# Rows of scores loaded in two parts, eight heads a round ahead, in a one-core talking-heads attention with a gated feed-forward behind it

## The chip, the core and the metric

The kernel runs on one core of a Trainium2 chip. The metric is the time of one execution on the device, in microseconds. TensorE does the matmuls and transposes, VectorE (DVE) and ScalarE (ACT) evict PSUM and do the element-wise work, GpSimd (POOL) helps, and SyncE (SP) issues nearly all DMA transfers, one after the other in the order of the program.

## The reference

Four batches, 12 heads, 448 rows, head size 64; then 1792 tokens through a feed-forward of 768 to 2048 to 768.

```python
scores = scale * np.matmul(q, k.transpose(0, 1, 3, 2))
scores = np.einsum('bhij,hg->bgij', scores, w_pre)
scores = scores - np.max(scores, axis=-1, keepdims=True)
attn = np.exp(scores)
attn = attn / (np.sum(attn, axis=-1, keepdims=True) + 1e-09)
attn = np.einsum('bhij,hg->bgij', attn, w_post)
attn_out = np.matmul(attn, v)
x = attn_out.transpose(0, 2, 1, 3).reshape(B * S, H * D)
h = x @ w_in
g = np.where(h >= 1, h, np.where(h <= -1, 0.0, (h + 1) ** 2 / 4))
out = g @ w_out
```

The two small matrices w_pre and w_post mix heads, so that the heads of one row of q must come together.

## The kernel before

**Attention, the first 440 us.** The rows of q are cut into 16 tiles: four a batch, of 120, 120, 120 and 88 rows. `scores` (L169) multiplies q and k for four heads of a tile at a time and evicts them to `ssb[t]`, which holds [row, head, column] for the whole tile; VectorE evicts two of the four heads (L187), ScalarE the other two (L189). A tile so takes three calls: heads 0 to 3, 4 to 7, 8 to 11.

To mix heads by a matmul, heads must lie on partitions. A *block* is 10 rows of a tile (a few have 9), taken with a stride. `load_s` (L198) moves one block by a DMA from SBUF to SBUF, from 10 partitions that hold 12 heads each to 120 partitions (row, head) of 448 columns:

```python
x = ap_.tile([KM, S], F32, tag="s10", name="s10", bufs=8)
nc.sync.dma_start(out=x[:ni * H], in_=ssb[t][o:n:nb])
```

`pre` (L214) multiplies the block by `wpre`, a 120x120 matrix with w_pre on ten diagonal places, either as one fp32 matmul (L223) or, for blocks that VectorE has split into a high and a low half (`split`, L205), as three faster ones (L221). A tile has 12 blocks, or 9 for the tile of 88 rows, in three *groups* of 4 (or 3): 48 groups. `row_max` (VectorE, L226), `exps` (ScalarE, L232), `norm` (GpSimd, L238 and L243, with a reciprocal on VectorE, L239) and `post` (TensorE, L260, evicted at L262) follow for each block, and `pv` (L296) multiplies by v.

**The loop (L893)** goes through the groups. Its round n, in program order, which is also the order of each engine's queue: load the rows of group n+1 (odd blocks first); "pre" of group n; the transposes planned in `at` (q and, at a batch's turn, k); the loads planned in `mid` (q, k) and the load of raw feed-forward weights (`conv_load`); the row maxima; the split of the first odd block of group n+1; `visit` (pv of an older tile); the exponentials; norm; copies of transposed q and k (`ql`, L166, reads the transposes' PSUM bank); the second split; "post" of group n-1; the conversion of weights (L373 to L377); the store of the weights converted a round ago (`conv_store`, L381); the score matmuls planned in `vis`; and what is planned in `late` (loads of q, load of the next batch's v, L130 and L133; the store of x, L340).

The score matmuls of tile t stand at the ends of rounds 3t-4, 3t-3 and 3t-2. The first group of tile t, group 3t, is loaded in round 3t-1 and is needed there by the first split: its rows can be moved only when the last four heads are evicted. k of the next batch is loaded in rounds 6 to 8 of each twelve and transposed a round later (L141, L149); v of the next batch is loaded in rounds 13 to 15 and the like. The PSUM pool `ps_l` has six banks in rotation, and s10 has eight buffers.

**The start (L758)** loads q, k, the head matrices and all three parts of v of batch 0, computes the scores of tile 0 and part of tile 1, makes `wpre`, `wpost` and the high and low halves of wpre on VectorE (L813 to L821), from a mask that GpSimd makes (L777 to L782), and enters the loop. Buffers of v's parts hold k's raw rows of batch 0 before.

**The feed-forward, from about 440 us to the end,** is not touched.

Of the kernel before, what the change touches and what calls it, by code (L numbers as in the profile page):

```python
# [9 lines left out]
F32 = mybir.dt.float32  # L10
# [12 lines left out]
def tile_talking_heads_moe(  # L23
# [11 lines left out]
    nc = tc.nc  # L35
# [159 lines left out]
    wr = {}  # L195
    aT = {}

    def load_s(m):  # L198
        t, o, ni, c = blocks[m]
        n, nb = tiles[t][2:]  # L200
        x = ap_.tile([KM, S], F32, tag="s10", name="s10", bufs=8)
        nc.sync.dma_start(out=x[:ni * H], in_=ssb[t][o:n:nb])
        s10[m] = x

    def split(m):  # L205
        k = blocks[m][2] * H
# [7 lines left out]
    def pre(m):  # L214

        k = blocks[m][2] * H
        lps[m] = ps_l.tile([KM, S], F32, tag="l", name="ps_l")
        x = s10.pop(m)
        if isinstance(x, tuple):
            for j, (w, y) in enumerate(((wpre_h, x[0]), (wpre_l, x[0]), (wpre_h, x[1]))):  # L220
                nc.tensor.matmul(out=lps[m], lhsT=w[:k], rhs=y[:k], start=(j == 0), stop=(j == 2))  # L221
        else:
            nc.tensor.matmul(out=lps[m], lhsT=wpre[:k], rhs=x[:k], start=True, stop=True)  # L223

    def row_max(m, nm):
        nc.vector.tensor_reduce(out=nm, in_=lps[m], axis=AX.X, op=ALU.max, negate=True)  # L226
# [156 lines left out]
    def conv(n, f):  # L383
        if n in CS and CS.index(n) < 2 * NF:
            f(CS.index(n))
# [372 lines left out]
    with tc.manual_schedule():  # L758
# [10 lines left out]
            load_k(0, hp, k0[hp // 2])  # L769
        load_q(1)  # L770
        wrep = ap_.tile([KM, H, IB], F32, tag="wr", name="wrep", bufs=8)
        wrep = wrep.rearrange("p h i -> p (h i)")[:, :2 * H].rearrange("p (n h) -> p n h", n=2)
        for n, w in enumerate((w_pre, w_post)):
            nc.sync.dma_start(out=wrep[:, n, :], in_=w.unsqueeze(0).to_broadcast([IB, H, H]))
        make_identity(nc, ident)

        mask = ap_.tile([KM, H, IB], F32, tag="wr", name="mask", bufs=8)[:, 0, :]  # L777
        nc.gpsimd.memset(mask, 1.0)
        nc.gpsimd.affine_select(out=mask, in_=mask, compare_op=ALU.is_ge, fill=0.0,
                                base=0, pattern=[[-H, IB]], channel_multiplier=1)  # L780
        nc.gpsimd.affine_select(out=mask, in_=mask, compare_op=ALU.is_ge, fill=0.0,
                                base=H - 1, pattern=[[H, IB]], channel_multiplier=-1)  # L782

        ps_w = pair()

# [8 lines left out]
        trans_q(0, 1)()()  # L794
        warm(4)
        trans_k(0, 1)()()
        for g in range(3):
            scores(0, [2 * g, 2 * g + 1], g == 1)
            if g < 2:
                for hp in range(2 * g + 2, 2 * g + 4):  # L800
                    trans_k(0, hp)()()
        for g in range(3):
            load_v(0, g)
        for g in range(2):
            trans_q(1, g)()()
        for m in groups[0]:
            load_s(m)
        wpre = ap_.tile([KM, KM], F32, name="wpre", bufs=1)
        wpost = ap_.tile([KM, H, IB], F32, name="wpost", bufs=1)
        wpre_h = ap_.tile([KM, KM], F32R, name="wpre_h", bufs=1)  # L810
        wpre_l = ap_.tile([KM, KM], F32R, name="wpre_l", bufs=1)

        nc.vector.scalar_tensor_tensor(  # L813
            out=wpre.rearrange("p (i g) -> p i g", g=H),
            in0=mask.unsqueeze(2).to_broadcast([KM, IB, H]), scalar=float(D) ** -0.5,
            in1=wrep[:, 0, :].unsqueeze(1).to_broadcast([KM, IB, H]), op0=ALU.mult, op1=ALU.mult)
        nc.vector.tensor_tensor(
            out=wpost, in0=wrep[:, 1, :].unsqueeze(2).to_broadcast([KM, H, IB]),
            in1=mask.unsqueeze(1).to_broadcast([KM, H, IB]), op=ALU.mult)
        nc.vector.tensor_copy(out=wpre_h, in_=wpre)  # L820
        nc.vector.tensor_tensor(out=wpre_l, in0=wpre, in1=wpre_h.bitcast(F32), op=ALU.subtract)  # L821
        scores(1, [0, 1], True)
        scores(1, [2, 3])
        at = {}
        mid = {}
        late = {}
# [3 lines left out]

        vis = {}
        vis2 = {}
        for g in range(2):
            put(0, lambda g=g: load_q(2, (g,)))
        for t in range(1, len(tiles)):
# [57 lines left out]
        for n in range(NG + 2):  # L893
            if n == NE:
                s_qk.close()
                s_se.close()
                pool['w'] = ctx.enter_context(tc.tile_pool(name="ffw", bufs=2, side="right",
                                                           reuse_waits="tile"))
                pool['ps_h'] = ctx.enter_context(tc.tile_pool(
                    name="ps_h", bufs=1, space=PSUM, side="right", reuse_waits="tile"))  # L900
            if n == NG - 1:
                s_ss.close()
            ms = groups[n] if n < NG else ()
            old = list(groups[n - 1]) if 0 < n <= NG else []
# [12 lines left out]
            for f in mid.pop(n, ()):  # L917
                f()
            conv(n + 1, conv_load)
            for m in ms:  # L920
                row_max(m, nm[:, m - ms[0]:m - ms[0] + 1])
            if n == NG - 1:
                w0_lo()
            if nxt:
                split(nxt.pop(0))
            rests = list(old)
            early = n < NE
            copies = visit(n, rests) if early else ()
            for j, m in enumerate(ms):
                if j == 3 and old and not early:  # L930
                    post(old.pop(0))
                exps(m, j, sm)
            conv(n, conv_scaled)
            if ms:
                norm(ms, sm)
            for f in (*turned, *copies):
                f()
            for m in nxt:
                split(m)
            if n == NG:  # L940
                step(0)
            for m in old:
                post(m)
            conv(n, conv_rest)
            conv(n - 1, conv_store)
            if not early:
                for f in visit(n, rests):
                    f()
            for t, hps in vis.pop(n, ()):
                scores(t, hps)  # L950
            for f in late.pop(n, ()):
                f()
# [155 lines left out]
```

## Time and profile before

| | |
|---|---|
| Timed executions | 870.63, 877.53 and 877.32 us; median 877.32 |
| The profiled execution | 873.21 us, of which the span (first to last instruction) is 871.5 |
| Mean granted TensorE clock | 0.998 |
| Busy share of the span | TensorE 98%, VectorE 74%, ScalarE 65%, GpSimd 24% |
| DMA | 162.47 MB, mean 186 GB/s |

A row of a timeline or wait view names the engine, the line of the kernel, the operation and the tiles (out<-in); a time in brackets is how long the engine sat idle just before, and what it was released by. SPq is SyncE's queue: its rows give the time in which transfers were issued, not in which they ran. PEld is the weight load of TensorE. In a table by windows, an engine's column is its busy time, and the PEclk column is the granted clock, where 1.00 is 2.4 GHz and 0.50 is 1.2 GHz.

### The profile page before, as it was taken

The page shows a single profiled execution, that of the slowest core. Times are in us where ns is not written, and L with a number is a line of the kernel's source. Part 1 is how long each engine was busy: PE and PEld are TensorE (multiplying, and loading weights), DVE is VectorE, ACT ScalarE, POOL GpSimd, SP SyncE. Part 2 cuts the span into 40 slices and gives each one's busy share as a digit, 9 for nine tenths or more (in the row PEclk, how much of TensorE's full clock was granted, in tenths as well). Part 3 has the DMA queues.
Part 4 walks back from the last instruction along what each step waited for, and adds up shares of the span by engine and source line. Part 5 has one row for each costly group of instructions (what it writes and reads, how often), then busy time and mean ns, then how long its engine had stood idle before and what let it go on. Part 6 is the DMA issues. An engine that isn't in the chain of part 4 may idle for free.

```text
span 871.5 us, 19952 instructions
## 1 busy us (share of the span) xinstructions
PE 854.1 (98%) x7848; PEld 734.2 (84%) x7848; DVE 645.1 (74%) x938; ACT 565.2 (65%) x1171; POOL 212.4 (24%) x269
## 2 busy tenths in 40 slices
PE   8999999999999999899999999999999999999998
PEld 6678777778787787687778788899999999999998
DVE  4887577775777767768578977997668978777853
ACT  3778788787887778778666466676667434433431
POOL 0366245653356533457320000000000000000000
PEclk9999999999999999999999999999999999999999
DMA  7888679986699876897556655654435544123331
GB/s 162 235 233 231 200 202 259 280 242 197 194 264 274 252 214 162 258 272 252 192 168 177 241 181 179 212 181 127 127 109 163 170 157 137 55 90 111 109 128 63
DMA packets 155329, 162.47 MB, mean 186 GB/s; under 512 B 66916, under 2 KB 148964, under 8 KB 155236
## 3 DMA queue, kind: packets, MB, share of 16 engines
q1 hardware_dynamic: 152404, 160.51, 61.1%
q8 instruction: 62, 1.02, 0.5%
q10 hardware_dynamic: 2832, 0.69, 0.4%
q14 instruction: 31, 0.25, 0.1%
HBM read 88.81 MB, written 33.82 MB: 141 GB/s over the span
## 4 chain that ended last, share of the span: by engine, by line
PE 86%; DMA 6%; DVE 3%; ACT 2%; SPq 2%; issue 1%; ACTq 0%; POOL 0%; DVEq 0%
PE ps_f L712 23%; PE ps_f L547 21%; PE ps_a L260 10%; PE ps_l L223 8%; PE ps_q L311 5%; DMA s<-ssb 5%; PE ps_l L221 5%; PE ps_q L180 3%; PE ps_s L180 3%; PE ps_r L276 2%; PE ps_q L306 1%; DMA k<-in_k_dram 1%; PE ps_t L161 1%; PE ps_k L141 1%; SPq L133 1%
## 5 line engine op out<-in xcount | busy, mean ns | idle before, releaser
L243 POOL TENSOR_SCALAR wr<-wpost,rs 120x120 f32<-120x120 f32 x180 | 141.4, 801 | 63.5 <-DVE rs L239 47.5
L232 ACT ACTIVATE e<-ps_l,nm 120x448 f32<-120x448 f32 x180 | 112.4, 632 | 60.9 <-DVE nm L226 59.6
L260 PE MATMUL ps_a<-wr,e 120*64 120x120 f32 (+1 forms) x2160 | 118.9, 266 | 0.0
L226 DVE TENSOR_REDUCE nm<-ps_l 120x1 f32<-120x448 f32 x180 | 105.7, 619 | 15.6 <-PE ps_l L223 11.4
L260 PEld LDWEIGHTS ps_a<-wr,e 120*64 120x64 f32 x2160 | 110.2, 137 | 2.6 <-issue 2.6
L695 ACT ACTIVATE sgh_p<-gq_p 128x1024 fp32r<-128x1024 f32 (+1 forms) x56 | 53.3, 953 | 89.7 <-PE ps_f L712 89.5
L223 PE MATMUL ps_l<-s,wpre 120*120 120x448 f32 x196 | 94.9, 569 | 5.8 <-DMA s<-ssb 3.8
L439 DVE SCALAR_TENSOR_TENSOR wl<-wi,wh 128x768 fp32r<-128x768 f32 x71 | 67.8, 954 | 41.9 <-ACT wh L436 41.9
L712 PE MATMUL ps_f<-wh,sgh_p 128*128 128x384 f32 x294 | 98.2, 334 | 0.0
L712 PE MATMUL ps_f<-wh,sgl_p 128*128 128x384 f32 x294 | 98.2, 334 | 0.0
L712 PE MATMUL ps_f<-wl,sgh_p 128*128 128x384 f32 x294 | 98.2, 334 | 0.0
L436 ACT ACTIVATE wh<-wi 128x768 fp32r<-128x768 f32 x71 | 59.7, 842 | 57.9 <-DVE wi L659 18.0
L262 ACT ACTIVATE aT<-ps_a 128x360 f32<-128x360 f32 x180 | 80.7, 494 | 13.7 <-PE ps_a L260 4.7
L696 DVE TENSOR_TENSOR sgl_p<-gq_p,sgh_p 128x1024 fp32r<-128x1024 f32 (+1 forms) x56 | 60.9, 1089 | 35.7 <-ACT sgh_p L695 35.7
L210 DVE CAST sh<-s 120x448 fp32r<-120x448 f32 (+1 forms) x82 | 33.2, 405 | 56.5 <-DMA s<-ssb 56.3
L187 DVE COPY ssb<-ps_q 120x896 f32<-120x896 f32 (+1 forms) x46 | 49.9, 1085 | 26.7 <-PE ps_q L180 26.7
L189 ACT ACTIVATE ssb<-ps_s 120x448 f32<-120x448 f32 (+1 forms) x96 | 47.2, 547 | 20.2 <-PE ps_s L180 17.8
L377 POOL TENSOR_TENSOR wt<-wt,wk 128x768 int32<-128x768 int32 x32 | 58.3, 1821 | 7.7 <-ACT wk L373 7.7
L221 PE MATMUL ps_l<-sh,wpre_h 120*120 120x448 f32 (+1 forms) x82 | 59.1, 721 | 0.0
L712 PEld LDWEIGHTS ps_f<-wh,sgl_p 128*128 128x128 f32 x294 | 55.2, 188 | 0.0
L712 PEld LDWEIGHTS ps_f<-wh,sgh_p 128*128 128x128 f32 x294 | 55.2, 188 | 0.0
L712 PEld LDWEIGHTS ps_f<-wl,sgh_p 128*128 128x128 f32 x294 | 55.2, 188 | 0.0
(235 smaller groups left out, 1943.3 us busy)
## 6 DMA issues: line engine op xcount, KB each, us to landing
s<-ssb SPq DMA_DIRECT2D x172, 210.0 KB
wraw<-in_moe_w_in_dram SPq DMA_DIRECT2D x16, 768.0 KB
wraw<-in_moe_w_out_dram SPq DMA_DIRECT2D x16, 768.0 KB
wi<-wod SPq DMA_DIRECT2D x29, 384.0 KB
wi<-wsd SPq DMA_DIRECT2D x28, 384.0 KB
wsd<-wt SPq DMA_DIRECT2D x16, 384.0 KB
wod<-wt SPq DMA_DIRECT2D x16, 384.0 KB
wi<-wss SPq DMA_DIRECT2D x16, 384.0 KB
```

The costliest lines, as they stand in the source:

```text
L221: nc.tensor.matmul(out=lps[m], lhsT=w[:k], rhs=y[:k], start=(j == 0), stop=(j == 2))
L223: nc.tensor.matmul(out=lps[m], lhsT=wpre[:k], rhs=x[:k], start=True, stop=True)
L226: nc.vector.tensor_reduce(out=nm, in_=lps[m], axis=AX.X, op=ALU.max, negate=True)
L232: nc.scalar.activation(out=e, in_=ps, func=AF.Exp, bias=nm, accum_out=sm[:, j:j + 1])
L243: nc.gpsimd.tensor_scalar_mul(out=w[:, :, :ni], in0=wpost[:, :, :ni], scalar1=rs[:, j:j + 1])
L260: nc.tensor.matmul(out=ps[half[s], r, :ni * H], lhsT=e[:, c0:c0 + 64], rhs=w[:, :, :ni], start=True, stop=True)
L262: nc.scalar.activation(out=a[:, :, :, c:c + ni], in_=ps[:, :, :ni * H].rearrange("q r (h i) -> q r h i", h=H), func=AF.Copy)
L436: nc.scalar.activation(out=hi, in_=t, func=AF.Copy, scale=2.0 ** -8)
L439: nc.vector.scalar_tensor_tensor(out=lo, in0=t, scalar=2.0 ** -8, in1=hi.bitcast(F32), op0=ALU.mult, op1=ALU.subtract)
L547: nc.tensor.matmul(out=o, lhsT=u[:, c, k], rhs=x, start=first and r == 0 and m == 0, stop=r == 2 and m == 2, skip_group_check=True)
L696: nc.vector.tensor_tensor(out=lo, in0=src, in1=hi.bitcast(F32), op=ALU.subtract)
L712: nc.tensor.matmul(out=o, lhsT=x[:, f, c], rhs=y[:, f % 2, :], start=first and f == 0 and m == 0, stop=hf == 1 and f == 3 and m == 2, skip ...
```

## The change

The *lead* groups are the first of each tile (0, 3, 6 and so on).

- A block of a lead group is loaded by two transfers: heads 0 to 7 (80 partitions) at the end of round 3t-2, behind that round's stores and loads, and heads 8 to 11 (40 partitions) at the place of the old load, in round 3t-1. All other groups are loaded as before.
- As the order of rows on the partitions is another one there, lead groups have a `wpre` of their own, made from two more loads of parts of w_pre (each some KB) and a mask of two more patterns, with halves of its own. The splits of both are made after the first scores of tile 1 and no longer before them.
- `conv_store` is written ahead of the row maxima, and what is in `late` ahead of the exponentials (up to round 43).
- At the start, only the first part of v is loaded before the loop; the other two are loaded in rounds 3 and 4, ahead of q's load.

```diff
-    def load_s(m):
+    lead = set(m for g in range(0, NG, 3) for m in groups[g])
+    EH = 8
+    EP = EH * IB
+
+    def load_s(m, early=False):
         t, o, ni, c = blocks[m]
         n, nb = tiles[t][2:]
-        x = ap_.tile([KM, S], F32, tag="s10", name="s10", bufs=8)
-        nc.sync.dma_start(out=x[:ni * H], in_=ssb[t][o:n:nb])
-        s10[m] = x
+        if m not in s10:
+            s10[m] = ap_.tile([KM, S], F32, tag="s10", name="s10", bufs=8)
+        x = s10[m]
+        if m not in lead:
+            nc.sync.dma_start(out=x[:ni * H], in_=ssb[t][o:n:nb])
+        elif early:
+            nc.sync.dma_start(out=x[:EP], in_=ssb[t][o:n:nb, :EH])
+        else:
+            nc.sync.dma_start(out=x[EP:], in_=ssb[t][o:n:nb, EH:])
...
+        for p, h in ((slice(0, EP), slice(0, EH)), (slice(EP, KM), slice(EH, H))):
+            nc.sync.dma_start(out=wrep[p, 2, :], in_=w_pre[h].unsqueeze(0).to_broadcast([IB, h.stop - h.start, H]))
...
         trans_k(0, 1)()()
+        load_v(0, 0)
         for g in range(3):
             scores(0, [2 * g, 2 * g + 1], g == 1)
+            if g == 1:
+                for m in groups[0]:
+                    load_s(m, True)
             if g < 2:
                 for hp in range(2 * g + 2, 2 * g + 4):
                     trans_k(0, hp)()()
-        for g in range(3):
-            load_v(0, g)
...
+        make_pre(True)
         nc.vector.tensor_tensor(
             out=wpost, in0=wrep[:, 1, :].unsqueeze(2).to_broadcast([KM, H, IB]),
-            in1=mask.unsqueeze(1).to_broadcast([KM, H, IB]), op=ALU.mult)
-        nc.vector.tensor_copy(out=wpre_h, in_=wpre)
-        nc.vector.tensor_tensor(out=wpre_l, in0=wpre, in1=wpre_h.bitcast(F32), op=ALU.subtract)
+            in1=masks[:, 0, :].unsqueeze(1).to_broadcast([KM, H, IB]), op=ALU.mult)
         scores(1, [0, 1], True)
         scores(1, [2, 3])
+        make_pre(False)
+        split_pre(False)
+        split_pre(True)
...
+        for g in (1, 2):
+            mid[g + 2] = [lambda g=g: load_v(0, g)]
...
             conv(n + 1, conv_load)
+            conv(n - 1, conv_store)
             for m in ms:
                 row_max(m, nm[:, m - ms[0]:m - ms[0] + 1])
...
             copies = visit(n, rests) if early else ()
+            if early:
+                for f in late.pop(n, ()):
+                    f()
...
             for m in nxt:
                 split(m)
+            if n + 2 < NG and (n + 2) % 3 == 0:
+                for m in (*groups[n + 2][1::2], *groups[n + 2][::2]):
+                    load_s(m, True)
             if n == NG:
                 step(0)
             for m in old:
                 post(m)
             conv(n, conv_rest)
-            conv(n - 1, conv_store)
```

## Rows read from the trace of the kernel before

**Rows 1.** The page, part 2: DMA share in 40 slices of the span.

```profile
DMA  7888679986699876897556655654435544123331
```

**Rows 2.** TensorE's waits, 0 to 440 us: total, times, longest.

```profile
PE ps_l L223 <- DMA s<-ssb: 3.8, 2, 2.3
```

**Rows 3.** VectorE's waits, 0 to 440 us.

```profile
DVE sh L210 <- DMA s<-ssb: 56.3, 33, 4.1
DVE ssb L187 <- PE ps_q L180: 26.7, 14, 3.3
```

**Rows 4.** Windows, rounds 2, 13, 14, 15, 17, 27, 36, 37: length, then columns below.

```profile
core 0: us, PE busy (x) PEld busy (x) DVE busy (x) ACT busy (x) POOL busy (x), PEclk, DMA share, GB/s
...
34.52:43.65 9.13, 7.98 (x92) 6.06 (x90) 6.17 (x13) 7.53 (x20) 4.21 (x7) 1.00 0.88 226
...
133.04:141.98 8.94, 8.94 (x124) 7.17 (x122) 7.48 (x15) 7.81 (x20) 6.01 (x7) 1.00 0.96 272
141.98:152.12 10.14, 9.40 (x123) 7.26 (x121) 5.84 (x12) 7.96 (x21) 4.16 (x6) 1.00 0.84 250
152.12:162.03 9.91, 8.71 (x119) 6.82 (x119) 7.35 (x14) 7.61 (x21) 6.19 (x7) 1.00 0.96 290
...
171.24:180.94 9.70, 9.49 (x123) 7.27 (x122) 6.51 (x13) 7.46 (x19) 5.21 (x7) 1.00 0.89 255
...
262.04:272.21 10.17, 8.70 (x119) 6.81 (x119) 7.23 (x14) 7.87 (x21) 5.97 (x7) 1.00 0.97 286
...
345.48:356.05 10.57, 8.23 (x104) 6.30 (x103) 6.90 (x13) 8.09 (x19) 4.49 (x5) 0.99 0.91 260
356.05:366.56 10.51, 10.51 (x121) 8.02 (x121) 8.14 (x15) 7.04 (x18) 6.27 (x8) 0.84 0.91 278
```

**Rows 5.** Timeline of SyncE's queue around round 14: start, duration of issue.

```profile
138.00 2.67 SPq L130 DMA_DIRECT2D v<-in_v_dram  x1
140.71 2.58 SPq L133 DMA_DIRECT2D v<-in_v_dram  x2
143.40 3.34 SPq L202 DMA_DIRECT2D s<-ssb  x4
```

**Rows 6.** Timeline of VectorE, round 14.

```profile
149.71 0.39 DVE L210 CAST sh<-s 120x448 fp32r<-120x448 f32 x1 [4.08 <-DMA s<-ssb]
...
150.76 0.50 DVE L166 TENSOR_TENSOR ql<-ps_t,qh 128x360 fp32r<-128x360 f32 x1
```

**Rows 7.** Timelines of SyncE's queue and of VectorE, round 11.

```profile
118.01 3.38 SPq L202 DMA_DIRECT2D s<-ssb  x4
...
120.80 0.40 DVE L210 CAST sh<-s 120x448 fp32r<-120x448 f32 x1 [0.85 <-DMA s<-ssb]
```

**Rows 8.** Waits of SyncE's queue, 0 to 440 us.

```profile
SPq L202 <- DVE ssb L187: 59.5, 15, 10.9
```

**Rows 9.** Timeline of SyncE's queue, round 8.

```profile
90.71 2.56 SPq L202 DMA_DIRECT2D s<-ssb  x3
...
94.21 1.96 SPq L114 DMA_DIRECT2D kraw<-in_k_dram  x2
...
98.61 0.63 SPq L115 DMA_DIRECT2D kraw<-in_k_dram  x1
```

**Rows 10.** Timeline of TensorE, round 9.

```profile
102.58 0.34 PE L149 MATMUL ps_k<-ident,kraw 64*128 64x64 f32 x2
```

**Rows 11.** The page, part 6: DMA issues of v, with the size of one.

```profile
v<-in_v_dram SPq DMA_DIRECT2D x12, 384.0 KB
...
v<-in_v_dram SPq DMA_DIRECT2D x24, 32.0 KB
```

**Rows 12.** Timeline of VectorE, the start and round 2.

```profile
22.13 0.28 DVE L821 TENSOR_TENSOR wpre_l<-wpre,wpre_h 120x120 fp32r<-120x120 f32 x1
...
24.67 2.88 DVE L226 TENSOR_REDUCE nm<-ps_l 120x1 f32<-120x448 f32 x4 [0.19 <-PE ps_l L223]
...
40.82 0.40 DVE L210 CAST sh<-s 120x448 fp32r<-120x448 f32 x1 [2.65 <-DMA s<-ssb]
```

More of the change, by code (lines that the diff above doesn't have):

```diff
@@ L218, in pre @@
         x = s10.pop(m)
+        wf, wh, wl = wpre[m in lead]
         if isinstance(x, tuple):
-            for j, (w, y) in enumerate(((wpre_h, x[0]), (wpre_l, x[0]), (wpre_h, x[1]))):
+            for j, (w, y) in enumerate(((wh, x[0]), (wl, x[0]), (wh, x[1]))):
                 nc.tensor.matmul(out=lps[m], lhsT=w[:k], rhs=y[:k], start=(j == 0), stop=(j == 2))
         else:
-            nc.tensor.matmul(out=lps[m], lhsT=wpre[:k], rhs=x[:k], start=True, stop=True)
+            nc.tensor.matmul(out=lps[m], lhsT=wf[:k], rhs=x[:k], start=True, stop=True)
     def row_max(m, nm):
@@ L771, in tile_talking_heads_moe @@
         wrep = ap_.tile([KM, H, IB], F32, tag="wr", name="wrep", bufs=8)
-        wrep = wrep.rearrange("p h i -> p (h i)")[:, :2 * H].rearrange("p (n h) -> p n h", n=2)
+        wrep = wrep.rearrange("p h i -> p (h i)")[:, :3 * H].rearrange("p (n h) -> p n h", n=3)
         for n, w in enumerate((w_pre, w_post)):
             nc.sync.dma_start(out=wrep[:, n, :], in_=w.unsqueeze(0).to_broadcast([IB, H, H]))
+        for p, h in ((slice(0, EP), slice(0, EH)), (slice(EP, KM), slice(EH, H))):
+            nc.sync.dma_start(out=wrep[p, 2, :], in_=w_pre[h].unsqueeze(0).to_broadcast([IB, h.stop - h.start, H]))
         make_identity(nc, ident)
[L777 to L782, printed above, removed]
+        masks = ap_.tile([KM, H, IB], F32, tag="wr", name="mask", bufs=8)[:, :3, :]
+        nc.gpsimd.memset(masks, 1.0)
+        for j, (p0, r) in enumerate(((0, H), (0, EH), (EP, H - EH))):
+            x = masks[:, j, :]
+            nc.gpsimd.affine_select(out=x, in_=x, compare_op=ALU.is_ge, fill=0.0,
+                                    base=-p0, pattern=[[-r, IB]], channel_multiplier=1)
+            nc.gpsimd.affine_select(out=x, in_=x, compare_op=ALU.is_ge, fill=0.0,
+                                    base=p0 + r - 1, pattern=[[r, IB]], channel_multiplier=-1)
+        nc.gpsimd.tensor_tensor(out=masks[:, 1, :], in0=masks[:, 1, :], in1=masks[:, 2, :], op=ALU.add)
         ps_w = pair()
@@ L807, in tile_talking_heads_moe, with make_pre, split_pre @@
             load_s(m)
-        wpre = ap_.tile([KM, KM], F32, name="wpre", bufs=1)
+        wpre = {x: [ap_.tile([KM, KM], F32 if i == 0 else F32R, name=f"wpre{x:d}{i}", bufs=1) for i in range(3)]
+                for x in (True, False)}
         wpost = ap_.tile([KM, H, IB], F32, name="wpost", bufs=1)
[L810 to L816, printed above, removed]
+        def make_pre(x):
+            mask, rep = (masks[:, 1, :], wrep[:, 2, :]) if x else (masks[:, 0, :], wrep[:, 0, :])
+            nc.vector.scalar_tensor_tensor(
+                out=wpre[x][0].rearrange("p (i g) -> p i g", g=H),
+                in0=mask.unsqueeze(2).to_broadcast([KM, IB, H]), scalar=float(D) ** -0.5,
+                in1=rep.unsqueeze(1).to_broadcast([KM, IB, H]), op0=ALU.mult, op1=ALU.mult)
+        def split_pre(x):
+            f, h, l = wpre[x]
+            nc.vector.tensor_copy(out=h, in_=f)
+            nc.vector.tensor_tensor(out=l, in0=f, in1=h.bitcast(F32), op=ALU.subtract)
+        make_pre(True)
         nc.vector.tensor_tensor(
             out=wpost, in0=wrep[:, 1, :].unsqueeze(2).to_broadcast([KM, H, IB]),
-            in1=mask.unsqueeze(1).to_broadcast([KM, H, IB]), op=ALU.mult)
-        nc.vector.tensor_copy(out=wpre_h, in_=wpre)
-        nc.vector.tensor_tensor(out=wpre_l, in0=wpre, in1=wpre_h.bitcast(F32), op=ALU.subtract)
+            in1=masks[:, 0, :].unsqueeze(1).to_broadcast([KM, H, IB]), op=ALU.mult)
         scores(1, [0, 1], True)
         scores(1, [2, 3])
+        make_pre(False)
+        split_pre(False)
+        split_pre(True)
         at = {}
```

## The prediction

> **What bounds the kernel now.** I read the page first: TensorE is busy for 98% of the span, and its clock is granted in full almost everywhere, so an edit that touches no matmul can only give back the moments in which TensorE waits. The change touches the attention rounds alone (the first 440 us), and there the DMA line of the page is to be seen at 5 to 9 tenths, mostly 6 to 9 [rows 1]. The waits of TensorE come next: by name only 3.8 us hang on rows of scores [rows 2]. VectorE waits for the same rows for 56.3 us in 33 waits [rows 3], but that is off TensorE's path as long as VectorE comes round in time. What it costs is read by stages. I cut the span into the 48 rounds of the loop (round n begins with the first matmul of its "pre"; "lead" groups, the first of each tile, are loaded in rounds 2, 5, 8 and so on), and the table [rows 4] shows length minus busy TensorE: 1.15 us idle in round 2, 0.74 in round 14, 1.20 in 15, 0.21 in 17, 1.47 in 27, 2.34 in 36. In round 37 nothing is idle, yet the granted clock is 0.84 and it takes 10.51 us where round 13, with the same work, takes 8.94: 1.57 us more right behind the longest idle time. The rest of the rounds keep TensorE full. So about 7 us of idle time, and 1.6 us of slow clock, is all that loads of rows can be blamed for, of a profiled execution of 873.21 us. That execution lies inside the three timed ones (870.63 to 877.53), 4.1 us under their median; I make the sum against it and don't add the 4.1.
>
> How a lead round loses its time is seen in round 14. SyncE's queue issues v's rows from 138.00 to 143.3 and four loads of lead rows from 143.40 to 146.74 [rows 5]. VectorE needs the first of the four at once, waits 4.08 us and starts at 149.71, that is 6.3 us after the issue; its next work, ql, frees a PSUM bank and ends at 151.26 [rows 6], and TensorE's second pair of score matmuls stands until then. In a round with an empty DMA queue the same load takes 2.8 us from issue to VectorE's start [rows 7]. So round 14's 6.3 us are 2.8 of the load and 3.5 of standing behind bulk, at 250 GB/s.
>
> **The change part by part.**
>
> *Two parts.* A lead load of 120 rows becomes one of 80, issued at the end of the round before, and one of 40. In 16 tiles that is 60 more issues on SyncE's queue (12 tiles of four blocks, 4 of three). An issue of these loads takes 0.84 us [rows 5, 7]; for a part I take the same (from below 0, should SyncE's cost go by size; no part is in the trace). SyncE has room where it stands idle until VectorE has evicted the last scores: 59.5 us in 15 such waits [rows 8]. There the early parts cost nothing, and the late one brings a third of the bytes. The bytes and rows are the same; what changes is the order. Before, the first block was whole after 210 KB. Now its late part comes behind the early parts of all four blocks: 560 + 70 KB, so 420 KB more are ahead of it. Where the queue was empty, these have long landed. Where it was full, they haven't: 430,000 bytes at round 15's 290 GB/s are 1.5 us. So the first split of a lead round moves between earlier by its whole wait and later by 1.5 us.
> In the rounds with an empty queue (5, 11, 23, 35 and their like) TensorE had no idle time, so a gain is worth 0. In round 14 the early parts sit in SyncE's order behind v's rows, exactly where the four loads stood; I take the late end, +1.5 us, and round 15 moves with it, since its idle time comes from the same late VectorE. Rounds 26 and 27 (same place, a batch later) would do the same, but round 27's idle time is a wait for rows that land when they land: arriving 1.5 us later it waits 1.5 us less. I take 0 for the pair, between -1.47 and +1.5. Rounds 17 and 29: 0, between -0.21 and +1.5 each. Round 2: 0, between its -1.15 and +1.5: its early parts sit behind the same raw weights as before, but 896 KB of v [rows 11] have left the queue ahead of these.
>
> *Batch turns (k's rows).* In round 8 SyncE is full: lead rows from 90.71, k's parts from 94.21 to 99.24 [rows 9]. Three more issues (this tile has three blocks) at 0.84 us push k's last part to 101.7; with 2.0 us from the end of an issue to use (2.8 less 0.84, rows 7) it is there at 103.7. TensorE transposes it at 102.58 [rows 10] with nothing in between that could go first: +1.2 us. VectorE's split comes 2.5 us later too; that is covered, since VectorE then stands waiting for TensorE before it evicts scores (26.7 us in 14 waits, rows 3). Three batches have this round, and the two later ones have more room between issue and transposes; so 1.2 us for the first and 0 for the others, bounds 0 and 3.6 (1.2 for each of the three).
>
> *v spread over steps.* Two of the three parts of v's first rows (each one load of 384 KB and two of 32 KB, rows 11) go from before 20 us, where nothing waited for them, to rounds 3 and 4. There TensorE is full, at a DMA share of about 0.9 like round 2's. 448 KB at round 2's 226 GB/s are 2.0 us of transfers a round, ahead of the weights and the next group's rows. The nearest rows are rounds 14 and 15, where the same parts came in the same place: 1.94 us idle together. Some of that is VectorE's slack: I take +1.0 us, between 0 and 4.0.
>
> *Bulk transfers.* The store of converted weights and the "late" edits are written earlier in the round, but on SyncE's own queue they keep their order: rows, q or k, weights in, weights out, v or x. Only the early rows are put behind. Cost 0; what it would gain is that it doesn't stand ahead of rows, and it didn't.
>
> *The start.* VectorE makes two operands and splits both: two splits and the second operand (five instructions of at most 0.28 us, as the one at 22.13) now stand between the last eviction and the first row maximum at 24.67 [rows 12]; two such are gone from before it. So the maxima come about 0.9 us later. That is hidden by round 2, where VectorE waits 2.65 us for rows at 40.82 [rows 12]; without that cover it would be +0.9. GpSimd's extra masks are made in its first instructions, long before VectorE reads them: 0.
>
> Sum: +1.5 (rounds 14, 15) + 1.2 (k) + 1.0 (v) = +3.7 us; 873.2 + 3.7 = **876.9 us**. With all low ends: -1.15 - 0.74 - 1.20 - 0.21 - 1.47 = -4.8 us, 868.4. With all high ends: +1.5 for each of rounds 2, 14, 17, 26, 29, +3.6 for k, +4.0 for v: +15 us, 888.
>
> The Trainium skill speaks against the split: "DMA: Bandwidth & Descriptors", section "Rules for kernel authors", says that two transfers to disjoint halves of the partitions are not worth it, because they share the same engines and serialize, and that one transfer should be used. The trace has no load in two parts to test it. By it the late part would gain nothing over the whole load anywhere and the 60 issues would remain; that is rival 2.
>
> **The rivals.**
> *1. The waits go.* If the early parts land before the last eviction also in full rounds, the first split waits only for 70 KB, and the idle times of rounds 2, 14, 15, 17 and 27 go: -4.8 us, 868.4; if round 36's wait and the slow clock behind it go too, 864.5. For it: VectorE's 56.3 us of waits. Against it: round 14's early parts are issued no sooner than the whole loads were.
> *2. The order hurts.* Everywhere the queue is full, the first block is whole 1.5 us later: five lead rounds (2, 14, 17 in rows 4; 26 and 29 read alike), +7.5, so 880.7. It decides from the point where VectorE's ql ends later than TensorE's first pair of score matmuls, and in round 14 that point is already passed. Where an idle time then reaches round 36's 2.3 us, the clock falls as in round 37, +1.57 each for rounds 2, 14 and 26: 885.4. With some of the k term it is past 886. For it: round 14. Against it: a late TensorE lets the queue drain, as assumed for round 27.
> *3. It doesn't do what it says.* Late parts wait as long as whole loads did, and no more: 873.2.
>
> **How the numbers follow.** The forecast 45%, rival 1 25%, rival 2 20%, rival 3 10%. One per cent, about what a measurement of this kernel can tell from no change, is 8.8 us: under 868.5 or over 886.1 against the median. Half of rival 1 lies under it, with a little for larger gains: 0.15; over it lies the worse half of rival 2 and a little for start and k together: 0.13; the rest is 0.72. The forecast's own range is 871 to 882; the range given, 868 to 885, leaves out rival 1's tail and rival 2's end.
>
> **What would show it.** Right: round 14's first split starts near 151 and the round grows to about 11.6 us; round 9 shows a wait of the k transposes for k's rows; rounds 3 to 5, where TensorE has no idle time now, show some; in round 11 the split's wait of 0.85 us is nearly gone and the round is as long as before. Wrong: idle times of rounds 2 and 14 gone, VectorE's 56.3 us of waits cut to a half or less; SyncE's issue of a part at half of 0.84. The prediction falls if SyncE's early parts are issued ahead of v's rows, or if TensorE's idle time before 440 us goes under 3 us.

## The result and the profile after

The kernel after takes 886.03 us (median of 4: 884.53 to 890.12), the kernel before beside it 875.35 (4: 870.63 to 877.53). The ratio is 1.0141, 95% interval 1.0096 to 1.0186: slower by 1.4%, 10.7 us. The forecast was 876.9 and no change, the range ended at 885: it was wrong, on the side of rival 2.

The profiled execution after took 890.12 us, the slowest of its four, where the one before took 873.21; its rounds show 16.8 of these 16.9 us, more than the medians' 10.7, so single rounds below are read for their pattern and not for the last tenth. The attention up to the same point (first matmul of round 46), by windows, before and then after:

```profile
0.00:436.44 436.44, 425.08 (x5314) 331.87 (x5315) 310.50 (x557) 332.74 (x832) 208.08 (x261) 1.00 0.79 229
```
```profile
0.00:453.27 453.27, 433.69 (x5314) 336.54 (x5314) 312.36 (x560) 335.73 (x832) 209.88 (x266) 0.98 0.76 221
```

The same 5314 matmuls. Length minus busy TensorE grew from 11.36 to 19.58 us (+8.2), and the matmuls themselves got longer by 8.6 us, at a granted clock of 0.98: half of the loss is waiting, half is slow clock behind it. The windows by rounds after (rounds 2, 14, 15, 17, 26, 27, 29 and 38; columns as in [rows 4]):

```profile
34.56:44.80 10.24, 8.29 (x89) 6.13 (x89) 6.53 (x15) 7.66 (x20) 4.56 (x7) 0.96 0.91 204
...
145.79:158.42 12.63, 9.99 (x123) 7.60 (x121) 6.66 (x13) 8.10 (x22) 4.77 (x5) 0.93 0.61 171
158.42:169.44 11.02, 11.02 (x119) 8.08 (x119) 8.30 (x15) 7.54 (x19) 7.16 (x8) 0.77 0.99 296
178.66:189.22 10.56, 9.42 (x123) 7.22 (x122) 5.74 (x12) 7.93 (x19) 4.24 (x6) 1.00 0.83 235
261.13:273.72 12.59, 9.85 (x124) 7.46 (x122) 6.45 (x13) 8.07 (x22) 4.56 (x5) 0.96 0.68 199
273.72:283.47 9.75, 9.75 (x120) 7.40 (x119) 7.94 (x14) 7.43 (x19) 6.52 (x8) 0.88 0.99 281
292.68:304.97 12.29, 10.02 (x123) 7.48 (x122) 6.52 (x13) 7.73 (x20) 5.19 (x6) 0.94 0.87 253
...
377.58:390.03 12.45, 9.98 (x123) 7.57 (x122) 6.06 (x12) 8.14 (x21) 3.81 (x5) 0.95 0.61 175
```

Rounds 26, 29 and 38 of the kernel before:

```profile
252.75:262.04 9.29, 9.29 (x124) 7.27 (x122) 5.64 (x11) 7.98 (x21) 3.96 (x6) 1.00 0.84 236
281.45:290.81 9.36, 9.36 (x123) 7.22 (x121) 6.45 (x14) 7.58 (x19) 5.15 (x7) 1.00 0.87 257
366.56:375.50 8.94, 8.94 (x123) 7.17 (x121) 6.50 (x13) 7.90 (x20) 4.06 (x4) 1.00 0.78 221
```

Against these and [rows 4]: round 14 has grown from 10.14 to 12.63 us with 2.64 idle, 26 from 9.29 to 12.59, 29 from 9.36 to 12.29, 38 from 8.94 to 12.45. All are lead rounds (3t-1). Rounds 15 and 27, right behind 14 and 26, have no idle time, but a granted clock of 0.77 and 0.88, a mean over stretches at 2.4 and at 1.2 GHz, behind 2.64 and 2.74 us in which TensorE stood: round 15's busy TensorE rose from 8.71 to 11.02 with the same work. The idle time of round 15 went (1.20 before), and its length grew all the same. The wait of round 36 and the slow round 37 of before are gone (8.14 and 8.94 us, nothing idle); in none of the later runs does round 36 stand idle for more than 0.5 us, so they belonged to that one execution.

Who waited, TensorE's and VectorE's waits after, 0 to 453 us ([rows 2, 3]):

```profile
PE ps_s L180 <- DVE ql L166: 13.8, 8, 2.7
DVE sh L220 <- DMA s<-ssb: 66.2, 29, 6.1
```

The first of these, before, 0 to 440 us:

```profile
PE ps_s L180 <- DVE ql L166: 1.0, 2, 0.7
```

TensorE's score matmuls wait for ql (1.0 us in 2 such waits before), and ql stands behind VectorE's split, which waits 66.2 us for rows (56.3 before), in fewer waits with a longest of 6.1. Round 14 in detail: SyncE's queue, VectorE, TensorE ([rows 5, 6]).

```profile
144.07 2.97 SPq L133 DMA_DIRECT2D v<-in_v_dram  x2
147.15 3.35 SPq L211 DMA_DIRECT2D s<-ssb  x4
150.88 0.77 SPq L213 DMA_DIRECT2D s<-ssb  x1
```
```profile
155.41 0.39 DVE L220 CAST sh<-s 120x448 fp32r<-120x448 f32 x1 [5.90 <-DMA s<-ssb]
...
156.46 0.50 DVE L166 TENSOR_TENSOR ql<-ps_t,qh 128x360 fp32r<-128x360 f32 x1
```
```profile
157.02 0.73 PE L180 MATMUL ps_s<-kh,qh 64*120 64x448 f32 x1 [2.64 <-DVE ql L166]
```

Round 14 begins at 145.79, so the late part is issued 5.09 us into the round, where the whole load before was issued 1.42 us into its round (143.40 less 141.98). From that issue to the split it takes 4.53 us (6.31 before). The sum, 9.62 us against 7.73, is what moved the split; ql starts 1.05 us behind it and the matmul 1.61 us. The cause of the late issue is the row above it: the four early parts occupy SyncE's queue for 3.35 us. But the 4.53 us are not those of an empty queue either (2.35 in round 11, below), so the late part also stands among the transfers.

In round 29 that second wait is all there is. The late part is issued 1.66 us into the round, earlier than the whole load before (2.13), and the split comes 7.76 us behind the issue instead of 4.86 (SyncE's queue and VectorE, before and then after):

```profile
283.58 3.38 SPq L202 DMA_DIRECT2D s<-ssb  x4
```
```profile
288.44 0.39 DVE L210 CAST sh<-s 120x448 fp32r<-120x448 f32 x1 [2.81 <-DMA s<-ssb]
```
```profile
294.34 4.07 SPq L213 DMA_DIRECT2D s<-ssb  x4
```
```profile
302.10 0.39 DVE L220 CAST sh<-s 120x448 fp32r<-120x448 f32 x1 [5.70 <-DMA s<-ssb]
```

What one issue takes, by line (whole blocks L209, early parts L211, late parts L213; duration in ns as min/median/max, then first and last start):

```profile
L209 SPq DMA_DIRECT2D s<-ssb x120: 768/794/1452, 23.6 to 451.2; - x120
```
```profile
L211 SPq DMA_DIRECT2D s<-ssb x60: 768/782/2911, 16.9 to 434.9; - x60
```
```profile
L213 SPq DMA_DIRECT2D s<-ssb x60: 762/767/899, 20.3 to 441.2; - x60
```

210, 140 or 70 KB: some 0.77 us, whatever the size. And SyncE stands idle in front of these loads much less: its wait for VectorE's last eviction, 59.5 us in 15 times before [rows 8], is now

```profile
SPq L213 <- DVE ssb L187: 14.0, 5, 4.1
```

In round 11, where the queues were empty, the split does come sooner ([rows 7]: wait 0.85, now 0.43; SyncE's queue, then VectorE), and the round takes 7.97 us as before:

```profile
121.38 3.22 SPq L213 DMA_DIRECT2D s<-ssb  x4
```
```profile
123.73 0.39 DVE L220 CAST sh<-s 120x448 fp32r<-120x448 f32 x1 [0.43 <-DMA s<-ssb]
```

The turn of k, round 8 (it begins at 92.54) and 9 (102.99), SyncE's queue and TensorE ([rows 9, 10]):

```profile
102.49 0.63 SPq L115 DMA_DIRECT2D kraw<-in_k_dram  x1
```
```profile
105.95 0.34 PE L149 MATMUL ps_k<-ident,kraw 64*128 64x64 f32 x2
```

k's last part is issued until 103.12, that is 10.58 us into round 8 (9.86 before), and its transposes don't wait. At the start the first row maxima begin 0.6 us later than before ([rows 12]: 24.67):

```profile
25.27 1.15 DVE L237 TENSOR_REDUCE nm<-ps_l 120x1 f32<-120x448 f32 x2
```

### The profile page after: what moved, and what is told of

It is laid out like the page before. It is cut to its first block, busy times and chain, and to the rows that moved or that the text cites. A ratio compares the mean times of both kernels' runs of the same rounds, so it can differ in the third digit from the quotient of the medians.

```text
span 888.4 us, 20049 instructions
## 1 busy us (share of the span) xinstructions
PE 862.7 (97%) x7848; PEld 738.9 (83%) x7848; DVE 646.9 (73%) x941; ACT 568.1 (64%) x1171; POOL 214.2 (24%) x274
## 4 chain that ended last, share of the span: by engine, by line
PE 74%; DMA 14%; DVE 5%; ACT 3%; SPq 2%; issue 1%; POOL 0%; ACTq 0%; DVEq 0%
PE ps_f L723 23%; PE ps_f L558 21%; DMA s<-ssb 9%; PE ps_a L271 7%; PE ps_l L234 6%; PE ps_q L322 4%; PE ps_l L232 3%; PE ps_s L180 3%; DMA v<-in_v_dram 2%; PE ps_q L180 2%; DMA wraw<-in_moe_w_in_dram 2%; ACT e L243 1%; PE ps_r L287 1%; PE ps_q L317 1%; DMA k<-in_k_dram 1%
## 5 line engine op out<-in xcount | busy, mean ns | idle before, releaser
L234 PE MATMUL ps_l<-s,wpre 120*120 120x448 f32 x196 | 98.6, 589 | 0.9 <-DMA s<-ssb 0.7
L220 DVE CAST sh<-s 120x448 fp32r<-120x448 f32 (+1 forms) x82 | 32.3, 394 | 66.6 <-DMA s<-ssb 66.2
L232 PE MATMUL ps_l<-sh,wpre 120*120 120x448 f32 (+1 forms) x164 | 78.8, 562 | 0.0
L232 PEld LDWEIGHTS ps_l<-sh,wpre 120*120 120x120 f32 (+1 forms) x164 | 31.6, 193 | 34.4 <-issue 29.7
```

What stands on the lines that cost most here:

```text
L234: nc.tensor.matmul(out=lps[m], lhsT=wf[:k], rhs=x[:k], start=True, stop=True)
```

## The experiments

Theory: the loss is the load in two parts alone; its price is SyncE's time (60 more issues, each as long as that of a whole block) wherever SyncE comes late to the rows, and the early parts' own turn among the transfers. Rivals: the move of v; the start; the bytes put ahead of the first block; the place of the early parts in SyncE's order. Every run has a ratio to the kernel before on the same chip.

**1. Whole blocks, the rest of the change kept.**

```diff
-    lead = set(m for g in range(0, NG, 3) for m in groups[g])
+    lead = set()
...
-            if g == 1:
-                for m in groups[0]:
-                    load_s(m, True)
...
-            if n + 2 < NG and (n + 2) % 3 == 0:
-                for m in (*groups[n + 2][1::2], *groups[n + 2][::2]):
-                    load_s(m, True)
```

> All of the change, but every block of a lead group is loaded whole at the old place (lead set empty, no early parts). Left out: only the two-part loads and what belongs to them. Order theory (the time comes from early parts standing ahead of the first late part, where the queue is full): 875 us, ratio to the kernel before 0.995 to 1.005, the first split of round 14 starts about 6.2 us after its load's issue again. Count theory (each transfer takes its turn of some 0.85 us on the queue, whatever its size): the same 875. Rival (v's rows moved into rounds 3 and 4, or stores and late loads written earlier in the round, cost the time): stays near 886, ratio 1.010 to 1.018.

874.31 us; ratio 1.0012 [0.9996, 1.0029]. All of the loss that can be told from no change is in the split. Its rounds 2, 4 and 5 by windows:

```profile
34.71:42.50 7.79, 7.79 (x91) 6.05 (x90) 6.38 (x14) 7.13 (x21) 5.04 (x10) 1.00 0.93 252
50.56:60.71 10.15, 9.55 (x123) 7.43 (x122) 7.46 (x15) 8.71 (x22) 4.54 (x5) 1.00 0.94 248
60.71:70.34 9.63, 9.41 (x121) 7.20 (x122) 6.43 (x13) 7.14 (x19) 5.13 (x7) 1.00 0.78 240
```

Round 2 takes 7.79 us instead of 9.13 (-1.34), and rounds 4 and 5, where v now arrives, 19.78 instead of 18.45 (+1.33). One profile's full rounds are loose, though, and these differences can't be put down to v: run 8, with v at the start, has 7.81 us in round 2, and run 10, with v moved as here, 18.44 in rounds 4 and 5. Rounds 14 to 16 took 31.7 us here and 29.3 before, with the same loads; rounds 26 and 38, with whole blocks in both runs, took 9.34 and 11.07 here, 11.21 and 9.93 in run 10. What holds is the total: the move of v costs nothing that shows.

**2. The two parts of v back at the start, blocks in two parts.**

```diff
+        for g in (1, 2):
+            load_v(0, g)
         for g in range(2):
             trans_q(1, g)()()
...
-        for g in (1, 2):
-            mid[g + 2] = [lambda g=g: load_v(0, g)]
```

> The changed kernel with the second and third part of v's first rows loaded before the loop again (behind the first q transposes). Order and count theory: only rounds 2 to 5 change, by 1 to 3 us: 883 to 886, ratio 1.009 to 1.013. Rival (v's move costs it): back to 875.

887.69 us; ratio 1.017 [1.0145, 1.0195]: above the 1.009 to 1.013 expected, and far from the rival's 875 us. Together with the split, v at the start costs in a place of its own: its six issues stand between the early and the late parts in SyncE's queue,

```profile
22.59 0.53 SPq L130 DMA_DIRECT2D v<-in_v_dram  x1
23.17 1.24 SPq L133 DMA_DIRECT2D v<-in_v_dram  x2
24.52 3.31 SPq L213 DMA_DIRECT2D s<-ssb  x4
```

and the late parts go at 24.52 instead of 20.34, so the loop begins at 27.46 instead of 23.55; rounds 2 to 5 then take 35.4 us, as before the change (35.6; 38.8 after it). From the late issue to the loop it takes 2.94 us, and 3.21 after the change: again SyncE's order, not bytes, sets the date.

**3. Four heads early instead of eight.**

```diff
-    EH = 8
+    EH = 4
```

> The changed kernel with 4 heads in the early part and 8 in the late one: the same number of transfers, in the full rounds 210 KB instead of 420 KB more ahead of the first whole block. Order theory, by bytes: half of the loss, 880 to 881, ratio about 1.006, the first split of rounds 14, 26 and 38 waits about 0.7 us less than in the changed kernel (5.9 there in round 14). Count theory: no less, 885 to 888, ratio 1.012 to 1.016, and the splits wait as long as in the changed kernel.

886.88 us; ratio 1.0147 [1.0109, 1.0186]. Half the early bytes, and in the total the same loss, as the count theory expected. The rounds don't all say so: in rounds 14, 26 and 38 the first split waits 5.00, 5.01 and 5.53 us, against 5.90, 6.07 and 5.81 after the change, and in the first two that is about the gain that the theory by bytes expected. Rounds 5, 20 and 27 lose instead (11.07, 12.31 and 12.04 us, against 10.40, 10.25 and 9.75). So the total speaks against bytes, and bytes are not excluded in a single round.

**4. Three pieces: the early part as two halves of the columns.**

```diff
-            nc.sync.dma_start(out=x[:EP], in_=ssb[t][o:n:nb, :EH])
+            for c in (slice(0, S // 2), slice(S // 2, S)):
+                nc.sync.dma_start(out=x[:EP, c], in_=ssb[t][o:n:nb, :EH, c])
```

> The changed kernel with each early part issued as two transfers of 224 columns: the same bytes in the same order, four (three) more transfers a lead round. Order theory by bytes: 886, ratio 1.012 to 1.016, as the changed kernel. Count theory: each lead round with a full queue waits another 3.4 us: seven such rounds, 905 to 910, ratio 1.033 to 1.040; SyncE's issues of a half piece take 0.84 us like those of a whole block.

915.61 us; ratio 1.0471 [1.0426, 1.0516]. The same bytes and times of need, 120 more issues than before instead of 60, and 4.7% instead of 1.4%, more than the 3.3 to 4.0% that the count theory gave. Round 14 (it begins at 157.76), SyncE's queue and VectorE:

```profile
158.67 8.01 SPq L212 DMA_DIRECT2D s<-ssb  x8
166.79 3.20 SPq L214 DMA_DIRECT2D s<-ssb  x4
```
```profile
169.15 0.39 DVE L221 CAST sh<-s 120x448 fp32r<-120x448 f32 x1 [7.75 <-DMA s<-ssb]
```

Eight issues take 8.0 us. From the late issue to the split it is then 2.36 us, less than in an empty round of before (2.8): in this round the queue adds nothing any more.

**5. The early parts issued by GpSimd.**

```diff
-            nc.sync.dma_start(out=x[:EP], in_=ssb[t][o:n:nb, :EH])
+            nc.gpsimd.dma_start(out=x[:EP], in_=ssb[t][o:n:nb, :EH])
```

> The changed kernel with the early parts issued from GpSimd's queue and not from SyncE's; the late parts stay. Issue theory (what costs is the 0.77 to 1.1 us that SyncE's queue takes for each early part, in rounds in which it is already late with v's or k's rows, so that the late parts are issued 3.4 to 4 us later): the loss goes, 871 to 876, ratio 0.995 to 1.003, and the first split of rounds 14, 26 and 38 waits about 4 us or less. Rival (the transfers themselves take their turn on the DMA engines, or the early parts' bytes stand ahead): it stays, 883 to 888.

884.21 us; ratio 1.0126 [1.0109, 1.0143]: not the issue theory's 871 to 876, but in the rival's band. Some lead rounds are near those of before (rounds 14 and 15 together 19.6 us against 20.05, round 29 9.20 against 9.36). Rounds 26 and 38 are not, with 12.11 and 11.82 us against 9.29 and 8.94, and the first split of rounds 14, 26 and 38 waits 4.91, 5.67 and 5.76 us where about 4 or less was expected. Most of the loss is round 2, which takes 16.07. There (it begins at 34.50) the early parts are issued behind GpSimd's scaling of round 1, after the late ones (which SyncE issues from 32.36 on), and are at VectorE 9.5 us later (GpSimd, VectorE):

```profile
34.91 2.45 POOL L254 TENSOR_SCALAR wr<-wpost,rs 120x120 f32<-120x120 f32 x4 [0.31 <-DVE rs L250]
37.31 2.31 POOL L211 DMA_DIRECT2D s<-ssb  x4
```
```profile
46.81 0.40 DVE L220 CAST sh<-s 120x448 fp32r<-120x448 f32 x1 [8.67 <-DMA s<-ssb]
```

Another queue with work of its own in front of the issue is no free queue.

**6. The early parts right behind "pre", ahead of the round's bulk.** The three lines that issue them move from the end of the round to the place behind `pre(m)`.

> The changed kernel with the early parts issued from SyncE right behind the round's pre, ahead of that round's q, weights, stores and v. Issue theory: the same issues, but some fall into times in which SyncE stands idle, and v's rows come 2 us later in front of the late parts: half of the loss, 877 to 882, ratio 1.003 to 1.009. Order theory by bytes (the early parts' 420 KB must land before the late one): 870 to 875.

882.73 us; ratio 1.011 [1.0082, 1.0139]: neither the issue theory's 1.003 to 1.009 nor the 870 to 875 us by bytes. By the points that is 0.3% less loss than in the kernel after, but the intervals overlap: the place in SyncE's order is not the main thing.

**7. Only the first odd block of a lead group in two parts** (15 more issues and not 60).

```diff
-    lead = set(m for g in range(0, NG, 3) for m in groups[g])
+    lead = set(groups[g][1] for g in range(0, NG, 3))
```

> The changed kernel with only the first odd block of a lead group, the one whose split comes first, in two parts; the other blocks are loaded whole at the old place. One more issue a tile in place of four (three). Issue theory: in full rounds the first whole block is there about as soon as in the kernel before (0.84 us later issued, 0.5 us less to move): 872 to 877, ratio 0.997 to 1.004.

874.35 us; ratio 1.0025 [1.0007, 1.0042]. This is the block that the first split needs. With a quarter of the issues the loss is nearly gone, and there is still no gain. The early bytes are a quarter too, so this run does not tell the two prices apart.

**8. Issues without bytes.** The kernel before, with four (or three) transfers of 80 partitions by 8 columns (2.5 KB) at the place where the change issues early parts. They go to a buffer that nothing reads.

```diff
+            if n + 2 < NG and (n + 2) % 3 == 0:
+                for m in groups[n + 2]:
+                    t, o, ni, c = blocks[m]
+                    tiny = ap_.tile([KM, 8], F32, tag="tiny", name="tiny", bufs=8)
+                    nc.sync.dma_start(out=tiny[:80], in_=ssb[t][o:tiles[t][2]:tiles[t][3], :8, :8])
```

> The kernel before, unchanged but for four (three) tiny transfers that SyncE issues at the place of the early parts: 80 rows of 8 columns into a tile that nobody reads, 2.5 KB each. Added work, nothing left out. Issue theory: if such an issue takes SyncE some 0.77 us too, the loss of the changed kernel comes back whole without its bytes: 882 to 890, ratio 1.010 to 1.019. Order theory by bytes: 874, ratio 0.998 to 1.003.

878.42 us; ratio 1.0053 [1.0036, 1.0071]. Round 20 (it begins at 201.12) takes 12.35 us where it took 10.24; SyncE's queue and VectorE there, and what one tiny issue takes:

```profile
200.46 2.53 SPq L944 DMA_DIRECT2D tiny<-ssb  x3
...
204.27 2.44 SPq L202 DMA_DIRECT2D s<-ssb  x3
```
```profile
208.98 0.39 DVE L210 CAST sh<-s 120x448 fp32r<-120x448 f32 x1 [4.20 <-DMA s<-ssb]
```
```profile
L944 SPq DMA_DIRECT2D tiny<-ssb x56: 768/784/2932, 32.2 to 421.2; - x56
```

In round 14 (it begins at 141.93) SyncE comes to the rows at 146.60, 4.67 us into the round and 3.25 later than before, and the split still comes no later (7.50 us into the round, 7.73 before):

```profile
149.43 0.39 DVE L210 CAST sh<-s 120x448 fp32r<-120x448 f32 x1 [3.85 <-DMA s<-ssb]
```

2.5 KB also take 0.78 us. The issue theory's 882 to 890 us did not come, and neither did the 874 by bytes: the issues alone, with next to no bytes, give 0.5% of the 1.3% that lie between the kernel after and run 1.

**9. Early parts by GpSimd, but those of the first two tiles by SyncE.**

```diff
-            nc.sync.dma_start(out=x[:EP], in_=ssb[t][o:n:nb, :EH])
+            q = nc.sync if t < 2 else nc.gpsimd
+            q.dma_start(out=x[:EP], in_=ssb[t][o:n:nb, :EH])
```

> The early parts of tiles 2 to 15 are issued by GpSimd, those of tiles 0 and 1 by SyncE as in the changed kernel. Theory of two bounds (SyncE's issue time, and the early parts' own turn among the transfers): round 2 is back at 10.2 us (16.07 with all parts from GpSimd), rounds 14, 15, 17 stay near the kernel before, rounds 26 and 38 stay at about 12 us, so 884.2 - 5.8 = about 878.4 us, ratio 1.004 to 1.008. Rival A, issue time alone: rounds 26 and 38 return to 9.3 and 9.0, ratio 1.002 or less. Rival B, parts cost the same from any queue: ratio 1.012 or more.

880.27 us; ratio 1.0089 [1.0058, 1.0119]. The point is just above the theory's 1.004 to 1.008 and its interval reaches from 1.006 to 1.012, so the size is not settled. Of the rounds named, 2 is back at 10.41 and 17 takes 9.67, as expected; 26 takes 13.48 and 38 11.95, against 9.29 and 8.94. Round 14 was to stay near the kernel before and takes 12.13, with 15 at 8.72 (together 20.85, against 20.05). Rival A falls. Round 14 (it begins at 144.50): SyncE's queue, GpSimd, VectorE, and the DMA issues from 144 to 157 us with the median time to landing:

```profile
146.05 3.35 SPq L214 DMA_DIRECT2D s<-ssb  x4
```
```profile
145.04 2.33 POOL L212 DMA_DIRECT2D s<-ssb  x4
```
```profile
154.22 0.39 DVE L221 CAST sh<-s 120x448 fp32r<-120x448 f32 x1 [6.08 <-DMA s<-ssb]
```
```profile
s<-ssb POOLq DMA_DIRECT2D x4, 140.0 KB, 7.2
```

Here the late part is issued 1.55 us into the round, as early as in run 1 (1.36), and yet the split comes 8.17 us behind the issue instead of 6.40: +1.8 us. In rounds 26 and 38 it is 8.08 against 5.06 and 8.15 against 6.82. The first split stands 9.72, 10.46 and 9.54 us into rounds 14, 26 and 38, and in the kernel after 9.62, 9.71 and 9.46: taking SyncE's time out did not bring these three rounds back. GpSimd issues the early parts there 0.54, 0.76 and 0.24 us into the round, sooner than SyncE did (1.36, 2.21 and 0.57), so it is not that it comes late. Rounds 17 and 29 do come back (9.67 and 9.21 us); for 29, whose late part was not issued late in the kernel after, no run shows why. A second price is left where the queue is full, and it reads as the early parts' own turn: 7.2 us from issue to landing.

**10. Two parts only in the rounds with an empty queue** (lead groups loaded in rounds 11, 23, 35).

```diff
-    lead = set(m for g in range(0, NG, 3) for m in groups[g])
+    lead = set(m for g in range(12, NG, 12) for m in groups[g])
```

> Only the lead groups loaded in rounds 11, 23 and 35 come in two parts, those where SyncE stood idle and the DMA queue was empty; all other groups whole, the rest of the change kept. Theory (where the split in two works there is nothing to win, as TensorE had no idle time there): ratio that of the version with whole blocks, 1.000 to 1.003; the first split of rounds 11, 23, 35 waits 0.3 to 0.5 us instead of 0.85 and these rounds stay at 7.97 us. Rival (an earlier split pays later in the tile): ratio 0.997 or less, rounds 11 to 13 shorter together by 0.4 us or more.

874.07 us; ratio 1.0008 [0.9988, 1.0027]. The split of round 11 waits 0.42 us, and rounds 11, 23 and 35 take 7.97, 7.97 and 7.96 us. Where the split works it is worth nothing.

**11. The kernel before, with each load of the next batch's v a round later and behind the rows.**

```diff
-                    put(w0, lambda t=t, g=g: load_v(tiles[t + 1][0], g))
+                    mid.setdefault(w0 + 1, []).append(lambda t=t, g=g: load_v(tiles[t + 1][0], g))
```

> The kernel before with one edit: each of the nine loads of the next batch's v is issued one round later and behind that round's first rows of scores, no block in two parts. Theory (what made round 14's first block late before was v's rows ahead of it on SyncE's queue and among the transfers): its first split starts 3 to 4 us after the issue instead of 6.3, the idle times of rounds 14, 15 and 27 (0.74, 1.20, 1.47) go, 873.2 - 3.4 = 869.8 us, ratio 0.995 to 0.998. Rival (bulk only meets the rows of the next round instead): rounds 15 and 16 take the stall over, ratio 1.000 or more.

873.25 us; ratio 1.0008 [0.9986, 1.003]. The theory's first half holds in part, its sum doesn't. Windows of rounds 14, 17, 26 and 29:

```profile
143.30:152.35 9.05, 9.05 (x124) 7.29 (x122) 6.05 (x12) 7.78 (x22) 4.16 (x5) 1.00 0.77 232
...
171.41:182.59 11.18, 9.52 (x123) 7.26 (x122) 7.06 (x14) 7.66 (x20) 5.76 (x7) 1.00 0.98 274
254.46:263.40 8.94, 8.94 (x123) 7.17 (x122) 6.28 (x12) 7.90 (x20) 4.04 (x5) 1.00 0.82 233
...
282.99:295.39 12.40, 10.05 (x124) 7.47 (x122) 7.50 (x15) 7.39 (x19) 6.21 (x7) 0.93 1.00 260
```

Rounds 14 and 26 get shorter (10.14 to 9.05, 9.29 to 8.94; the split of 14 starts 4.99 us behind the issue, not 6.31 and not the 3 to 4 expected), the idle times of rounds 15 and 27 stay (1.16 and 1.51 us), and rounds 17 and 29, the next lead rounds, take them over (9.70 to 11.18, 9.36 to 12.40). The rival was right with its sum and wrong with its place: rounds 15 and 16 stayed as they were. No version here beats the kernel before.

## Why the prediction was wrong

- **What bounds the kernel** held: TensorE, held up by ql behind VectorE's first split. The wait of the score matmuls for ql grew from 1.0 to 13.8 us, more than the 8.2 us of new idle time (other waits went).
- **The step that failed is the cover of SyncE's issue time, and the zeros beside it.** The text priced an early part's issue at 0.84 us, which held (0.78), and then covered it: "SyncE has room where it stands idle ... 59.5 us in 15 such waits", "There the early parts cost nothing". In rounds 14 and 26 SyncE comes to the rows straight from v's loads and has no such room, and in round 38 it stood idle for 1.8 us; the early parts' 3.3 to 3.8 us of issues push the late part from 1.42 to 5.09 us into round 14, from 2.11 to 5.67 in 26 and from 1.11 to 5.01 in 38. I read the sum of SyncE's waits and not the waits of the rounds that lose time, which I had done for VectorE and TensorE. That issues cost time by themselves is shown by runs 4 and 8: more of them without more bytes cost 4.7% in the one and 0.5% in the other.
- **It is not the whole loss.** Run 9, with SyncE's early issues gone for 14 of 16 tiles, still loses 0.9% (0.6 to 1.2), and rounds 14, 26 and 38 with it. By these points some 0.5% is SyncE's time, and the larger part goes with the early parts' own turn among the transfers, which the text priced at 1.5 us for one pair of rounds and at 0 for the others. What sets this second price, bytes, the number of transfers or GpSimd's way of issuing, no run here shows.
- **Round 14's +1.5 us** was near in size (the split came 1.9 us later in its round, the round took 2.5 longer), and single profiles bear out its mechanism for this round: in run 8 SyncE's issues without bytes delay the split by nothing, in run 9 the early parts without SyncE's issues delay it by 2.0 us. Behind the late part's issue the delay against run 1 is 1.8 us there, and 3.0 and 1.3 in 26 and 38. In the kernel after it looks different: the late part is issued later, and the stretch behind the issue got shorter (6.31 to 4.53), probably as early parts landed while the late one waited to be issued. So the two prices don't add up in full: what the late part spends waiting for its issue, it doesn't spend in the queue.
- **The zeros for rounds 2, 17, 26, 27 and 29** are most of the rest of the sum. They took +1.11, +0.86, +3.30, -0.42 and +2.93 us, round 38, which the text did not name, +3.51, and rounds 3, 5, 30 and 39 to 41, not named either, 5.3 together. ("The rest of the rounds keep TensorE full" overlooked 0.69 us in round 39, which changes no term.) For round 27, "arriving 1.5 us later it waits 1.5 us less" failed at the clock: its idle time did go (1.47 to 0), but its matmuls took 9.75 instead of 8.70 us at a granted clock of 0.88. The same in round 15. The prediction had this price in rival 2 only, at 1.57 us a round and only behind 2.3 us of idle time; round 15 alone paid 2.31 behind 2.64, round 27 1.05 behind 2.74, and round 3, behind 1.95, 0.89 at a clock of 0.86.
- **k, +1.2 us: did not come.** The three more issues (2.5 us) pushed k's last part by 0.7 us against its round, as SyncE issues the early parts from the round's start on, where it had stood waiting: its rows went out 1.33 us into round 8 before. Here the cover that the text claims did exist, and the text did not use it.
- **v, +1.0 us:** not to be seen. Run 1's total (ratio up to 1.0029) leaves at most 2.5 us for v, start and bulk together. Its rounds 4 and 5 took 1.33 us more than before and its round 2 1.34 less, but run 10, with the same loads, shows nothing in rounds 4 and 5 (18.44 us, 18.45 before), so both are within the scatter of single rounds.
- **The start and the bulk:** nothing that shows, within the same 2.5 us; the maxima came 0.6 and not 0.9 us later. **Round 11** went as forecast.
- **Rival 2** had the side and nearly the size (880.7 to 885.4), by bytes ahead of the first block in five lead rounds, without round 38 and without SyncE's time. Run 3's total speaks against bytes and its rounds 14 and 26 for them, so part of that nearness may be luck. The Trainium skill's rule on two transfers to disjoint partition halves ("DMA: Bandwidth & Descriptors", section "Rules for kernel authors"), cited ahead of the result, points the right way, and run 9 fits its reason, shared engines: 1.8 us more behind the issue in round 14. In the section "Issuing engines are not separate DMA queues" the same page of the Trainium skill says that the time to initiate a DMA is usually small beside the DMA itself; in this case the trace has 0.77 us of issue against 2.8 us from issue to use, more than a quarter, and run 8 shows that 56 such issues cost 0.5%.

What stays open: what the early parts' own turn is made of (see above), how the loss divides exactly, as runs 8 and 9 give it by one version each with intervals of 0.4 to 0.7% and 0.6 to 1.2%, and why round 2's early parts took 9.5 us from GpSimd in run 5. None of these was tried by itself.

## What to carry to other kernels

Count a split transfer twice. In issues: here each cost its 0.77 us of SyncE's queue whatever its size, and the part that is needed last is issued behind all the others. And in what it puts ahead of that part among the transfers: it cost time here even where another engine issued it. Look for the cover in the very round that is on the path, not in the engine's sum of waits. Don't count on a later, emptier wait to give back an idle time of TensorE: here the clock fell behind idle times of 1.95 to 2.74 us, and the next round lost again.

## What the runs showed that was not expected

- A transfer between partitions takes SyncE 0.77 us to issue at 210, 140, 70 and 2.5 KB alike, while one of v's 384 KB loads takes 0.53 in run 2's first row, and a median of 0.48 over the twelve of the kernel before (0.37 to 2.67).
- Half of the 16.8 us of the profiled loss is matmuls at a lower granted clock: 8.6 us for the same 5314 matmuls, behind idle times of 1.95 to 2.74 us.
- Moving bulk by one round (run 11) moved the stall to the next lead round almost in full: in this part of the kernel the DMA share stands at 0.77 to 1.0, and the sum hardly depends on which round pays.
